# Small array tiles for a linear-attention state, and two vector steps moved to GpSimd

## The chip, the cores and the metric

The kernel runs on one NeuronCore of one Trainium2 chip. A core has engines that run their own instruction queues side by side: TensorE (PE, with its weight loads PEld) for matrix products, VectorE (DVE), ScalarE (ACT), GpSimd (POOL), and SyncE (SP), which issues DMA transfers here. On-chip operands lie in SBUF; matrix products land in PSUM. The metric is the device time of one launch in microseconds, lower is better. Arrays are f32 at the interface.

## The reference

Four layers run one after the other on x of 2048 tokens by 512 columns, each as x + layer(layernorm(x)): layers 1 and 3 are softmax attention with 32 heads of 16 columns, layers 2 and 4 a linear attention with learned features ("hedgehog"). Both kinds use the same weights in both places.

```
def _B_ref(x, wqkv, w_phi, wo):
    qkv = (x @ wqkv).reshape(B, S, 3, H, Dh) ...
    pq = einsum("bhsd,hdf->bhsf", q, w_phi)
    pk = einsum("bhsd,hdf->bhsf", k, w_phi)
    phi_q = concatenate([softmax(pq), softmax(-pq)], axis=-1)
    phi_k = concatenate([softmax(pk), softmax(-pk)], axis=-1)
    kv  = einsum("bhsf,bhsd->bhfd", phi_k, v)
    z   = einsum("bhsf->bhf", phi_k)
    num = einsum("bhqf,bhfd->bhqd", phi_q, kv)
    den = einsum("bhqf,bhf->bhq", phi_q, z)[..., None] + 1e-6
    return (num / den).transpose(0, 2, 1, 3).reshape(B, S, D) @ wo
```

So in a linear layer every head has 32 features per token (16 from softmax(p), 16 from softmax(-p)), and a state of 32 x 17: 16 columns of v and one of ones, which gives the denominator. Here S = 2048, H = 32, Dh = 16.

## The kernel before, in words

Two classes hold the layers: `LayerA` (softmax) and `LayerB` (linear). The program is layer 1 (`a1`), 2 (`b1`), 3 (`a2`), 4 (`b2`). Weights are folded and split into two f16 parts once, beside layer 1, and kept in DRAM. Tokens go in four blocks `j` of 512, each of four tiles `t` of 128. A further path for very large scores (`LayerAny`) stands behind a branch that is not taken.

A linear layer has three stages. In `feed` (L1051), for each of the 16 token tiles, PE makes pk, pq and the values in PSUM (36 matmuls of 128x512, L1064). `expo` (L1119) takes the maximum and the minimum per head (L1124, L1125), writes x - max and min - x side by side into `f` (L1127, L1128), all on DVE, and ACT takes the exponential of both (L1129). `part_sums` (L1132) forms the inverse row sums on DVE (L1135, L1136, L1138), and `share` (L1141) multiplies by them on Pool (L1144). For k, `halves` (L1146) splits the result into two f16 parts: ACT the high one (L1150), Pool the low one (L1151). PE adds the tile's product of features and values to the state in `gather` (L1178). For q, `turn` (L1169) transposes on PE and copies by ACT. The value tile `vt` is a new buffer for each token tile, with two memsets on Pool (L1068, L1069). Tiles 0 to 9 of a linear layer also carry the end of the softmax layer before it: pieces of its output projection, its residual sums, the statistics of the next norm (small Pool instructions, L406 to L423), and one norm step a tile (L446, L456, L459).

When the last tile is in, `blocks` (L1186) copies the state from PSUM into `kvb`: two tiles of 4 groups of 128 columns, zero apart from four 32x17 blocks on the diagonal of each group. `heads(j)` (L1198) multiplies it with the transposed features of a block: 8 f32 matmuls of 128x128 against 512 tokens (L1204), two groups in each double bank of PSUM. `norm2` (L525) brings each double bank out: ACT copies (L528), DVE transposes in 32x32 blocks (L530), DVE adds the small constant and inverts (L532, L533), DVE multiplies (L535), and `finish_o` (L516) transposes back on DVE (L518), ACT takes the high half (L522), Pool the low half (L523). `rest` runs heads 0 and 1; `finish` (L1215) runs the output projection (L559, L585), the residual sum (L575), heads 2 and 3 and, in layer 2, the first part of layer 3.

Who sets the order: within `feed` of the linear layer all compute engines follow the program as written; in `rest` and `finish` DVE, ACT and Pool, and in layer 4's `finish` PE also, stand in an order that a planner makes from its own costs. SyncE's queue is ordered by the planner everywhere. PSUM has three double banks under the name "S" (one holds the state during `feed`) and two single banks.

Layers 1 and 3 begin with octet 0 of the heads; the weights of octet 1 are loaded by `octet_w` (L624). In L272 to L274 and L809 to L811 this stands ahead of `load_head`, which loads the row operands for the first scores; `feed_end` (L825) loads the remaining rows and the shift row.

Of the kernel before, what the change touches and what calls it, by code (L numbers as in the profile page):

```python
# [50 lines left out]
def mha_hedgehog_stack(ctx, tc, x_in, a_wqkv, a_wo, b_wqkv, b_wphi, b_wo, out, shmin=SHMIN):  # L51
# [14 lines left out]
    def big(shape, dt, name):  # L66
        return bigp.tile(shape, dt, tag="big", name=name)
# [94 lines left out]
    def prep_a():  # L162
# [38 lines left out]
        with tc.manual_schedule(engines=COMPUTE):  # L201
            a1.begin((w0, v0))
            ln.stats(0, 2, True)
            ln.stats(2, 2, True)
            mk = [peak_of(flat(wk), 0, nc.scalar)]
            ln.scaled(0), ln.scaled(1)
            ps01, ps23 = bank2(), bank2()
            ln.transposed(0, 2, ps01)
            mk += [peak_of(flat(wk), 1, nc.scalar), peak_of(flat(wq), 0, nc.scalar), peak_of(flat(wq), 1, nc.vector)]
            ln.scaled(2), ln.scaled(3)  # L210
            ln.high(0, 2, ps01)
            ln.transposed(2, 2, ps23)
            ln.high(2, 2, ps23)
            es, sc = scale_from(mk, "sA")
            con["scA"] = sc
            high0(w0[:, :, 1], wk, sc), high0(w0[:, :, 0], wq, sc)
            stats1 = lns[1].stats_parts(0, 4)
            next(stats1)
            low0(w0[:, :, 1], wk, sc)
            run(stats1)  # L220
            low0(w0[:, :, 0], wq, sc)
            con["qk"] = cp.tile([P, 1], F32, name="c_qk")
            nc.vector.tensor_scalar(con["qk"], es, QS / 8192.0, None, op0=ALU.mult)
            con["q1"] = cp.tile([P, 1], F32, name="c_q1")
            nc.vector.tensor_scalar(con["q1"], es, 1.0 / 8192.0, None, op0=ALU.mult)
            ln.low(0, 2, ps01)
            ln.low(2, 2, ps23)
            mv = [peak_of(flat(wv), u, nc.scalar) for u in range(2)]
            pj = {ten: bank2()[:, 0, :] for ten in (1, 0)}
            gens = {ten: a1.project(0, 0, pj[ten], ten) for ten in (1, 0)}  # L230
            for ten in (1, 0):
                for _ in range(4):
                    next(gens[ten])
            run(gens[1]), run(gens[0])
            lns[1].scaled(0), lns[1].scaled(1)
            con["esA"], con["scAv"] = scale_from(mv, "sAv")
            high0(v0, wv, con["scAv"])
            lns[1].scaled(2), lns[1].scaled(3)
            a1.head_evac(0, 1, pj[1])
            low0(v0, wv, con["scAv"])  # L240
            a1.head_evac(0, 0, pj[0], False)
            nc.sync.dma_start(dA[0], w0)
            nc.sync.dma_start(dAv[0], v0)
            for j in range(1, NJ):
                ln = lns[j]
                ps01, ps23 = bank2(), bank2()
                ln.transposed(0, 2, ps01)
                ln.transposed(2, 2, ps23)
                ln.high(0, 2, ps01)
                ln.high(2, 2, ps23)  # L250
                a1.head_square(j - 1, 0)
                if j == 1:
                    lns[2].stats(0, 4)
                ln.low(0, 2, ps01)
                ln.low(2, 2, ps23)
                if j < NJ - 1:
                    a1.head_values(j - 1)
                nxt = [lambda t=t: lns[j + 1].scaled(t) for t in range(4)] if j + 1 < NJ else []
                if j == 1:
                    octet(1)  # L260
                for f in nxt:
                    f()
                if j > 1:
                    octet(j)
                if j == 2:
                    a1.head_norms(0)
                a1.head(j, (1,))
                if j + 2 < NJ:
                    lns[j + 2].stats(0, 4)
                a1.head(j, (0,), j == NJ - 1)  # L270
                octet_low(j)
                if j == 2:  # L272
                    a1.next_w = a1.octet_w(1)
                    a1.load_head()  # L274
            a1.feed_end()

# [71 lines left out]
    def prep_rest():  # L348

        yield from prep_ao()  # L350
        while len(folded) < 2:
            yield
        es, sc = scale_from((yield from peaks(folded)), "sB")
        con["pB"] = cp.tile([P, 1], F32, name="c_pB")
        nc.vector.tensor_scalar(con["pB"], es, 1.0 / 8192.0, None, op0=ALU.mult)
        for i in range(2):
            yield from split_parts(folded[i], sc, f"bhl{i}", dBqk[:, i])
        wv = load_w(b_wqkv[:, 1024:1536], "bwv")
        yield from landing()
        esv, scv = scale_from((yield from peaks([wv])), "sBv")  # L360
        yield from split_parts(wv, scv, "bhlv", *[dBv[a] for a in range(2)])

        wo = big([P, NC4, 512], F32, "bwo")
        for h in range(4):
            for q in range(2):
                r = h * 32 + q * DH
                nc.sync.dma_start(wo[r:r + DH], b_wo.rearrange("(c q h d) n -> q h d c n", q=2, h=4, d=DH)[q, h])
        yield from landing()
        eso, sco = scale_from((yield from peaks([wo])), "sBo")
        yield from split_parts(wo, sco, "bhlo", dBo)  # L370
        con["oB"] = out_scale(esv, eso, "c_oB")
# [153 lines left out]
    def norm2(ps, dst):  # L525

        raw = pp.tile([P, 2 * 512], F32, tag="p", name="raw")
        nc.scalar.activation(raw, ps.rearrange("p q t -> p (q t)"), AF.Copy)  # L528
        yt = pp.tile([P, 2, 16, 32], F32, tag="p", name="yt2")
        nc.vector.transpose(yt.rearrange("p q a b -> p (q a b)"), raw)  # L530
        rec = sp.tile([P, 2, 16], F32, name="rec2", bufs=2)
        nc.vector.tensor_scalar(rec, yt[:, :, :, 16], 1e-6 * KS, None, op0=ALU.add)  # L532
        nc.vector.reciprocal(rec, rec)  # L533
        yn = np_.tile([P, 16, 32], F32, tag="yn", name="yn2", bufs=5)
        nc.vector.tensor_tensor(yn.rearrange("p a (q d) -> p q a d", q=2), yt[:, :, :, 0:16],  # L535
                                rec.unsqueeze(3).to_broadcast([P, 2, 16, 16]), ALU.mult)
        finish_o(yn, dst)

# [77 lines left out]
    class LayerA:  # L616
# [179 lines left out]
        def feed(self, lns, work):  # L796

            for j, (a, b, c) in enumerate(work):
# [8 lines left out]
                    self.head_norms(0)  # L807
                self.head(j)
                if j == 2:  # L809
                    self.next_w = self.octet_w(1)  # L810
                    self.load_head()  # L811
                if 0 < j < NJ - 1:
                    self.head_values(j - 1)
# [11 lines left out]
        def feed_end(self):  # L825
            self.head_norms(1)
            self.head_bound(2)
            self.load_shift(0, slice(0, AHEAD), None, (1,))
            self.load_rows(0, slice(AHEAD, S), self.kq_end)
            self.head_values(2)  # L830
            self.head_norms(2)
            self.head_bound(3)
# [202 lines left out]
    class LayerB:  # L1035
# [3 lines left out]
        def begin(self):  # L1039
# [6 lines left out]
                self.wv.append(t)  # L1046
            self.kvp = None
            self.latek = self.lateq = None
            self.qT, self.obs = [], []

        def feed(self, j, xnT, between=lambda t: None):  # L1051

# [4 lines left out]
            for t in range(4):  # L1057
# [6 lines left out]
                            nc.tensor.matmul(dst, xnT[:, a, c, t * P:(t + 1) * P], w(b, c),  # L1064
                                             start=(i == 0 and c == 0), stop=(i == 2 and c == NC4 - 1))

                vt = np_.tile([P, 2, H, 17], F16, tag="yn", name="vt", bufs=5)
                nc.gpsimd.memset(vt[:, 0, :, 16:17], 1.0)  # L1068
                nc.gpsimd.memset(vt[:, 1, :, 16:17], 0.0)  # L1069
                bank = lambda name: psS.tile([P, 2, 512], F32, tag="S", name=name)[:, 0, :]  # L1070
                last = tt == NT - 1
                pk = bank("pk")
                project(pk, lambda b, c: self.wqk[:, 1, b, c, :])
                if last:
                    f_k = self.expo(pk)
                    self.kvb = [np_.tile([P, 4, P], F32, tag="yn", name="kvb", bufs=5) for _ in range(2)]
                    for kvb in self.kvb:
                        nc.gpsimd.memset(kvb, 0.0)
                else:
                    pq = bank("pq")  # L1080
                    project(pq, lambda b, c: self.wqk[:, 0, b, c, :])
# [37 lines left out]
        def expo(self, ps):  # L1119
# [5 lines left out]
            nc.vector.tensor_reduce(mn, pf, AX.X, ALU.min)  # L1125
            f = pp.tile([P, H, 2, DH], F32, tag="p", name="f")
            nc.vector.tensor_tensor(f[:, :, 0, :], pf, mx.unsqueeze(2).to_broadcast([P, H, DH]), ALU.subtract)  # L1127
            nc.vector.tensor_tensor(f[:, :, 1, :], mn.unsqueeze(2).to_broadcast([P, H, DH]), pf, ALU.subtract)  # L1128
            nc.scalar.activation(f, f, AF.Exp, scale=con["pB"])  # L1129
            return f  # L1130

# [53 lines left out]

        def blocks(self):  # L1186

            for i, kvb in enumerate(self.kvb):
                for h in range(4):
                    r = 32 * h  # L1190
                    dst = kvb[r:r + 32, :, r:r + 17]
                    src = self.kvp[r:r + 32, i, 0:272].rearrange("p (g e) -> p g e", g=4)[:, :, h * 17:h * 17 + 17]
                    if i:
                        nc.scalar.activation(dst, src, AF.Copy)
# [1 line left out]
                        nc.vector.tensor_copy(dst, src)  # L1196

        def heads(self, j):  # L1198
            ob = big([P, NC4, 2, 512], F16, f"obB{j}")
            for o in range(4):  # L1200
                ps = psS.tile([P, 2, 512], F32, tag="S", name="pn")
                for par in range(2):
                    g = 2 * o + par
                    nc.tensor.matmul(ps[:, par, :], self.kvb[g // 4][:, g % 4, :], self.qT[j][g // 4][:, g % 4, :], start=True, stop=True)  # L1204
                norm2(ps, ob[:, o])
            self.obs.append(ob)

        def rest(self):
# [193 lines left out]
```

## Time and profile before

| what | us |
|---|---|
| median of three runs | 2550.31 |
| lowest and highest run | 2549.44, 2551.63 |
| the profiled execution | 2549.26 |
| its span in the trace | 2547.5 |
| PE busy | 2447.8 |
| ACT busy | 2177.5 |
| DVE busy | 974.0 |
| POOL busy | 379.0 |

The profile is of one execution. Rows of the page and of the groups give line, engine, operation, output and inputs, shapes and count, then busy time, mean ns of one, and the engine's idle time just before with what ended it. Rows in order of time begin with the start and the length in us from the start of the span. L1144 is line 1144 of the kernel before. The granted clock of the profiled execution was 0.99 of full speed.

### The profile page before, as it was taken

What the parts mean: (1) busy time and instruction counts of PE and PEld (TensorE: products, weight loads), DVE (VectorE), ACT (ScalarE), POOL (GpSimd) and SP (SyncE); (2) the same over time, 40 slices, a digit from 0 to 9 for tenths busy, and PEclk for the clock granted to TensorE, in tenths of its full rate; (3) what the DMA queues carried; (4) which work ended last, traced back from release to release, by engine and by line L of the source; (5) the groups of instructions that cost most, each with busy time, mean ns of one, the idle gap of its engine ahead of it and who ended that gap; (6) DMA issues with size and microseconds to landing.
All of it is one profiled execution on the core that took longest, in us unless ns stands there. A gap on an engine that the chain in (4) does not pass through costs nothing.

```text
span 2547.5 us, 50724 instructions
## 1 busy us (share of the span) xinstructions
PE 2447.8 (96%) x20960; PEld 761.2 (30%) x20960; DVE 974.0 (38%) x1884; ACT 2177.5 (85%) x2437; POOL 379.0 (15%) x523
## 2 busy tenths in 40 slices
PE   6799999999999999999899999999999999998998
PEld 3222222222232222345343222222222222224543
DVE  6212211212133316899871122112122111459897
ACT  5699999999999999644438999999999999993552
POOL 2100000101000000266430010000010000005552
PEclk9899999999999999999999999999999999999999
DMA  3510230033033612100224003202300351110003
GB/s 141 104 44 5 43 47 6 14 50 78 1 79 66 222 51 84 50 17 6 70 96 68 14 6 50 40 1 45 65 2 10 71 140 41 67 67 26 9 17 109
DMA packets 109650, 135.29 MB, mean 53 GB/s; under 512 B 63408, under 2 KB 64672, under 8 KB 107232
## 3 DMA queue, kind: packets, MB, share of 16 engines
q1 hardware_dynamic: 108736, 129.59, 20.7%
q8 instruction: 166, 2.72, 0.4%
q0 software_dynamic: 672, 2.36, 0.2%
q14 instruction: 76, 0.62, 0.1%
HBM read 60.06 MB, written 39.85 MB: 39 GB/s over the span
## 4 chain that ended last, share of the span: by engine, by line
PE 78%; DVE 11%; ACT 5%; issue 3%; POOL 2%; SPq 1%; DMA 0%; ACTq 0%; POOLq 0%; DVEq 0%
PE pv L891 37%; PE s L877 21%; PE pqk L585 6%; PE po L585 5%; ACT p L880 3%; DVE su L1135 2%; PE pbv L1064 1%; PE pk L1064 1%; PE pq L1064 1%; DVE f L1127 1%; POOL f L1144 1%; DVE f L1128 1%; DVE mx L1124 1%; PE pst L446 1%; DVE su L1136 1%
## 5 line engine op out<-in xcount | busy, mean ns | idle before, releaser
L880 ACT ACTIVATE p<-s 128x1024 f32<-128x1024 f32 x2048 | 1887.8, 1116 | 20.2 <-PE s L877 17.7
L891 PE MATMUL pv<-p,v 128*32 128x512 f32 x8192 | 1091.9, 605 | 2.6 <-DVE yt L503 1.8
L877 PE MATMUL s<-kq 49*128 49x512 f16 x3872 | 606.1, 382 | 20.3 <-DMA kq<-sh 12.0
L877 PEld LDWEIGHTS <-kq 49*128 49x128 f16 x3968 | 136.8, 94 | 637.4 <-issue 625.3
L891 PEld LDWEIGHTS pv<-p,v 128*32 128x32 f32 x8192 | 161.8, 108 | 397.3 <-issue 367.2
L687 POOL TENSOR_TENSOR sq<-stg 128x512 bf16<-128x512 f16 x48 | 70.1, 1460 | 1043.1 <-DVE stg L761 940.2
L503 DVE STREAM_TRANSPOSE yt<-pv 128x512 f32<-128x512 f32 x64 | 45.8, 716 | 452.9 <-PE pv L891 441.0
L760 DVE TENSOR_SCALAR tq<-pqk,c_qk 128x512 f32<-128x512 f32 x48 | 35.9, 749 | 445.0 <-PE pqk L585 411.8
L1144 POOL TENSOR_TENSOR f<-f,su 128x1024 f32<-128x1024 f32 x62 | 119.8, 1933 | 386.0 <-DVE su L1138 351.6
L1064 PEld LDWEIGHTS <-xnTa 128*128 128x128 f16 x1152 | 110.6, 99 | 150.8 <-DVE f L1128 23.6
L585 PEld LDWEIGHTS <-wA 128*32 128x32 f16 (+1 forms) x2496 | 86.6, 97 | 200.8 <-issue 175.2
L573 DVE SCALAR_TENSOR_TENSOR xt<-po,c_oA,xt 128x512 f32<-128x512 f32 x64 | 47.1, 735 | 233.9 <-PE po L585 223.5
L585 PE MATMUL pqk<-xnTb,wA 128*32 128x512 f16 (+1 forms) x1248 | 116.9, 379 | 2.2 <-ACT xnTb L456 2.2
L585 PE MATMUL pqk<-xnT,wA 128*32 128x512 f16 (+1 forms) x1224 | 110.9, 379 | 3.1 <-ACT xnT L456 2.5
L1064 PE MATMUL pbv<-wbv,xnTa 128*128 128x512 f16 x384 | 92.9, 394 | 19.0 <-DVE f L1128 19.0
L1129 ACT ACTIVATE f<-f,c_pB 128x1024 f32<-128x1024 f32 x64 | 72.7, 1148 | 42.3 <-DVE f L1128 42.2
L1150 ACT ACTIVATE fk<-f 128x1024 f16<-128x1024 f32 x30 | 31.7, 1057 | 73.6 <-POOL f L1144 73.6
L585 PE MATMUL po<-woA,ob 128*32 128x512 f16 x1152 | 92.3, 379 | 0.0
L1064 PE MATMUL pk<-wbqk,xnTa 128*128 128x512 f16 x384 | 88.5, 379 | 0.0
L1064 PE MATMUL pq<-wbqk,xnTa 128*128 128x512 f16 x384 | 88.4, 379 | 0.0
L1135 DVE TENSOR_REDUCE su<-f 128x64 f32<-128x1024 f32 x64 | 77.5, 1211 | 9.2 <-ACT f L1129 8.5
L1176 ACT ACTIVATE qT<-pqt 128x512 f32<-128x512 f32 x64 | 34.6, 593 | 52.0 <-PE pqt L1175 52.0
(280 smaller groups left out, 1930.1 us busy)
## 6 DMA issues: line engine op xcount, KB each, us to landing
kq<-stg SPq DMA_DIRECT2D x168, 128.0 KB
xd<-xt SPq DMA_DIRECT2D x40, 512.0 KB
xt<-xd SPq DMA_DIRECT2D x40, 512.0 KB
v<-vyt SPq DMA_DIRECT2D x384, 16.0 KB
oD<-osp SPq DMA_DIRECT2D x24, 256.0 KB
ob<-oD SPq DMA_DIRECT2D x8, 768.0 KB
xt<-in_A_x_dram SPq DMA_DIRECT2D x8, 512.0 KB
wbqk<-dBqk SPq DMA_DIRECT2D x2, 2048.0 KB
```

The costliest lines, as they stand in the source:

```text
L503: nc.vector.transpose(yt.rearrange("p a b -> p (a b)"), ps)
L573: nc.vector.scalar_tensor_tensor(xt[:, u, :], ps, co, xt[:, u, :], op0=ALU.mult, op1=ALU.add)
L585: nc.tensor.matmul(ps[r, :], w[:, r], x, start=(n == 0), stop=(n == of - 1), skip_group_check=cols)
L687: nc.gpsimd.tensor_tensor(sq, hi, hi, ALU.mult)
L760: nc.vector.tensor_scalar(tq, ps, cqk, CLAMP, op0=ALU.mult, op1=ALU.min)
L877: nc.tensor.matmul(s[:, u, :], self.side(g, half, r, 0, kt * P, P), self.side(g, half, r, 1, j * 512, 512), start=True, stop=True)
L880: nc.scalar.activation(pt, s, AF.Exp, scale=0.25 / (QS * QS))
L891: nc.tensor.matmul(acc[32 * hh:32 * hh + 32, :], self.oct[o]["v"][:, r:r + 32], pt[:, hh % 2, :], start=(kt == 0), stop=(kt == NT - 1), sk ...
L1064: nc.tensor.matmul(dst, xnT[:, a, c, t * P:(t + 1) * P], w(b, c), start=(i == 0 and c == 0), stop=(i == 2 and c == NC4 - 1))
L1129: nc.scalar.activation(f, f, AF.Exp, scale=con["pB"])
L1135: nc.vector.tensor_reduce(su, f[:, r, :], AX.X, ALU.add)
L1144: nc.gpsimd.tensor_tensor(f3, f3, self.part_sums(f3, slice(0, 64), factor), ALU.mult)
```

## The change

Five edits stand together.

1. The state is kept as 8 groups of 32 columns in one `kvb` tile, not as diagonal blocks. `heads` takes the features in two halves; each half is 16 matmuls of a 32x32 array tile, a different one for each, written to two double banks of PSUM at once. The order of heads that comes out is another, so the rows of `wo` are loaded in that order, by 16 transfers in place of 8.
2. min - x is formed on Pool in two steps: min - max of 32 columns, then that minus (x - max), which DVE has written to SBUF.
3. The product with the inverse sums in `norm2` is on Pool.
4. The value tiles rotate over three buffers, whose constant columns are written once per layer.
5. The call that loads the next octet's weights is moved out of the loops and into `feed_end`, behind the rows' loads.

```diff
@@ prep_a, LayerA.feed
                 if j == 2:
-                    a1.next_w = a1.octet_w(1)
                     a1.load_head()
@@ feed_end
             self.load_rows(0, slice(AHEAD, S), self.kq_end)
+            self.next_w = self.octet_w(1)
             self.head_values(2)
@@ prep_rest
-        for h in range(4):
-            for q in range(2):
-                r = h * 32 + q * DH
-                nc.sync.dma_start(wo[r:r + DH], b_wo.rearrange("(c q h d) n -> q h d c n", q=2, h=4, d=DH)[q, h])
+        for i in range(4):
+            for c in range(4):
+                r = 32 * c + DH * (i % 2)
+                nc.sync.dma_start(wo[r:r + DH, i // 2:4:2, :],
+                                  b_wo.rearrange("(k h d) n -> h d k n", k=2, d=DH)[4 * ((c - i) % 4) + i])
@@ norm2
-        nc.vector.tensor_tensor(yn.rearrange("p a (q d) -> p q a d", q=2), yt[:, :, :, 0:16],
+        nc.gpsimd.tensor_tensor(yn.rearrange("p a (q d) -> p q a d", q=2), yt[:, :, :, 0:16],
                                 rec.unsqueeze(3).to_broadcast([P, 2, 16, 16]), ALU.mult)
@@ LayerB.feed
-                vt = np_.tile([P, 2, H, 17], F16, tag="yn", name="vt", bufs=5)
-                nc.gpsimd.memset(vt[:, 0, :, 16:17], 1.0)
-                nc.gpsimd.memset(vt[:, 1, :, 16:17], 0.0)
+                if tt < 3:
+                    self.vts.append(np_.tile([P, 2, H, 17], F16, tag="yn", name="vt", bufs=5))
+                    nc.gpsimd.memset(self.vts[tt][:, 0, :, 16:17], 1.0)
+                    nc.gpsimd.memset(self.vts[tt][:, 1, :, 16:17], 0.0)
+                vt = self.vts[tt % 3]
...
-                    self.kvb = [np_.tile([P, 4, P], F32, tag="yn", name="kvb", bufs=5) for _ in range(2)]
-                    for kvb in self.kvb:
-                        nc.gpsimd.memset(kvb, 0.0)
+                    self.kvb = np_.tile([P, 8, 32], F32, tag="yn", name="kvb", bufs=5)
+                    nc.gpsimd.memset(self.kvb, 0.0)
@@ expo
             nc.vector.tensor_tensor(f[:, :, 0, :], pf, mx.unsqueeze(2).to_broadcast([P, H, DH]), ALU.subtract)
-            nc.vector.tensor_tensor(f[:, :, 1, :], mn.unsqueeze(2).to_broadcast([P, H, DH]), pf, ALU.subtract)
+            nc.gpsimd.tensor_tensor(mn, mn, mx, ALU.subtract)
+            nc.gpsimd.tensor_tensor(f[:, :, 1, :], mn.unsqueeze(2).to_broadcast([P, H, DH]), f[:, :, 0, :], ALU.subtract)
@@ blocks
-                    dst = kvb[r:r + 32, :, r:r + 17]
+                    dst = self.kvb[r:r + 32, 4 * i:4 * i + 4, 0:17]
@@ heads
-            for o in range(4):
-                ps = psS.tile([P, 2, 512], F32, tag="S", name="pn")
-                for par in range(2):
-                    g = 2 * o + par
-                    nc.tensor.matmul(ps[:, par, :], self.kvb[g // 4][:, g % 4, :], self.qT[j][g // 4][:, g % 4, :], start=True, stop=True)
-                norm2(ps, ob[:, o])
+            for k in range(2):
+                ps = [psS.tile([P, 2, 512], F32, tag="S", name="pn") for _ in range(2)]
+                for g in range(4):
+                    for i in range(4):
+                        c = 32 * ((i + g) % 4)
+                        r = slice(32 * i, 32 * i + 32)
+                        nc.tensor.matmul(ps[i // 2][c:c + 32, i % 2, :], self.kvb[r, 4 * k + g, :],
+                                         self.qT[j][k][r, g, :], start=True, stop=True, skip_group_check=True)
+                for p in range(2):
+                    norm2(ps[p], ob[:, 2 * k + p])
```

More of the change, by code (lines that the diff above doesn't have):

```diff
@@ L809, in feed @@
                 if j == 2:
-                    self.next_w = self.octet_w(1)
                     self.load_head()
@@ L1048, in begin @@
             self.latek = self.lateq = None
-            self.qT, self.obs = [], []
+            self.qT, self.obs, self.vts = [], [], []
         def feed(self, j, xnT, between=lambda t: None):
@@ L1186, in blocks @@
         def blocks(self):
-            for i, kvb in enumerate(self.kvb):
+            for i in range(2):
                 for h in range(4):
                     r = 32 * h
-                    dst = kvb[r:r + 32, :, r:r + 17]
+                    dst = self.kvb[r:r + 32, 4 * i:4 * i + 4, 0:17]
                     src = self.kvp[r:r + 32, i, 0:272].rearrange("p (g e) -> p g e", g=4)[:, :, h * 17:h * 17 + 17]
```

## The prediction, made before the result was known

> **What bounds the kernel now.** I read the page first, then tables of stretches for the two linear layers, then one token tile in order of time, the groups of instructions, and the chain that ended last. In every row of a group the last two numbers are busy us and mean ns, then idle time.
>
> ```profile
> span 2547.5 us, 50724 instructions
> PE 2447.8 (96%) x20960; PEld 761.2 (30%) x20960; DVE 974.0 (38%) x1884; ACT 2177.5 (85%) x2437; POOL 379.0 (15%) x523
> ```
>
> The averages mislead. The two softmax layers, some 2,000 us, are not touched: in the built program their PE instructions stand in the same order. All that changes lies in the linear layers: layer 2 from about 1047 to 1348 us, layer 4 from 2297 to the end. I call the moment at which DVE starts the first row sum of token tile t (su, L1135) its mark. The table cuts layer 2 at the marks of tiles 0, 1, 2, 3, 4, 5, 9, 14 and 15, and adds the stretch of the first normalisations. Columns: length, then busy us and count of PE, PEld, DVE, ACT, POOL.
>
> ```profile
> 1052.62:1062.23 9.61, 8.81 (x51) 4.17 (x44) 9.51 (x16) 4.81 (x6) 6.28 (x5) 1.00 0.00 0
> 1062.23:1078.17 15.94, 13.19 (x105) 6.68 (x104) 13.15 (x22) 6.24 (x9) 8.98 (x19) 0.89 0.12 45
> 1078.17:1087.78 9.61, 9.40 (x63) 4.55 (x60) 9.51 (x15) 4.67 (x6) 6.28 (x5) 1.00 0.10 37
> 1087.78:1101.06 13.28, 10.51 (x77) 5.28 (x76) 13.04 (x23) 4.92 (x6) 9.38 (x20) 0.89 0.11 41
> 1101.06:1111.40 10.34, 10.34 (x73) 5.52 (x71) 9.28 (x15) 4.95 (x7) 6.27 (x5) 0.98 0.00 0
> 1111.40:1155.83 44.43, 40.46 (x291) 22.53 (x290) 38.52 (x61) 22.98 (x30) 25.06 (x20) 1.00 0.04 13
> 1155.83:1202.54 46.71, 46.65 (x335) 24.76 (x334) 45.16 (x72) 22.86 (x28) 31.37 (x25) 1.00 0.00 1
> 1202.54:1209.92 7.38, 6.27 (x51) 3.13 (x49) 5.04 (x9) 3.87 (x5) 4.04 (x3) 1.00 0.13 36
> 1216.00:1246.00 30.00, 27.88 (x101) 12.58 (x100) 29.82 (x52) 15.92 (x24) 11.59 (x11) 1.00 0.10 36
> ```
>
> Tiles 9 to 13 are plain: PE is busy 46.65 of 46.71 us, 9.34 us a tile. Tiles 5 to 8 also carry a piece of the norm; they take 11.11 us, and neither PE nor DVE is full. In the last row DVE is full. One tile of the 11.11 us kind:
>
> ```profile
> 1122.52 1.21 DVE L1135 TENSOR_REDUCE su<-f 128x64 f32<-128x1024 f32 x1
> ...
> 1124.35 0.20 DVE L1138 TENSOR_SCALAR su<-su 128x64 f32<-128x64 f32 x1
> ...
> 1124.69 1.93 POOL L1144 TENSOR_TENSOR f<-f,su 128x1024 f32<-128x1024 f32 x1 [4.43 <-DVE su L1138]
> ...
> 1126.65 1.06 ACT L1150 ACTIVATE fk<-f 128x1024 f16<-128x1024 f32 x1 [2.39 <-POOL f L1144]
> ...
> 1127.03 1.94 POOL L1144 TENSOR_TENSOR f<-f,su 128x1024 f32<-128x1024 f32 x1 [0.41 <-DVE su L1136]
> 1127.62 0.58 ACT L456 ACTIVATE xnTa<-pst 128x512 f16<-128x512 f32 x1
> ...
> 1128.23 0.69 DVE L459 TENSOR_TENSOR xnTa<-pst,xnTa 128x512 f16<-128x512 f32 x1 [1.37 <-ACT xnTa L456]
> ...
> 1128.92 2.13 POOL L1151 TENSOR_TENSOR fk<-f,fk 128x1024 f16<-128x1024 f32 x1
> ...
> 1130.03 0.68 DVE L1127 TENSOR_TENSOR f<-pk,mx 128x512 f32<-128x512 f32 x1
> 1130.63 0.68 DVE L1128 TENSOR_TENSOR f<-mn,pk 128x512 f32<-128x512 f32 x1
> ...
> 1131.34 1.15 ACT L1129 ACTIVATE f<-f,c_pB 128x1024 f32<-128x1024 f32 x1 [0.36 <-DVE f L1128]
> ...
> 1133.62 1.21 DVE L1135 TENSOR_REDUCE su<-f 128x64 f32<-128x1024 f32 x1
> ```
>
> The loop: row sums (DVE), share of k (POOL), high half (ACT), norm copy (ACT, DVE), then four DVE steps on the next tile's k, exponential (ACT), next mark. Pool's three instructions of the tile are in order; the last ends 1131.05, 8.53 us behind the mark. Nothing of the next tile needs Pool until its own mark, so this end is harmless today.
>
> **The change part by part.**
>
> ```profile
> L1144 POOL TENSOR_TENSOR f<-f,su 128x1024 f32<-128x1024 f32 x62 | 119.8, 1933 | 386.0 <-DVE su L1138 351.6 <-DVE su L1136 28.5 <-PE po L585 5.9
> L1204 PE MATMUL pn<-qT,kvb 128*128 128x512 f32 x128 | 59.5, 610 | 8.2 <-ACT raw L528 6.0 <-DVE xt L575 1.5 <-DVE kvb L1196 0.7
> L523 POOL TENSOR_TENSOR obB<-yb,obB 128x512 f16<-128x512 f32 x32 | 37.2, 1162 | 68.2 <-ACT obB L522 68.2
> L535 DVE TENSOR_TENSOR yn<-yt,rec 128x512 f32<-128x512 f32 x32 | 26.4, 824 | 0.0
> L1128 DVE TENSOR_TENSOR f<-mn,pq 128x512 f32<-128x512 f32 x32 | 21.7, 677 | 0.0
> L406 POOL TENSOR_TENSOR lu<-ly 128x2 f32<-128x2 f32 x36 | 8.3, 231 | 21.5 <-DVE ly L397 19.1
> ```
>
> min - x. DVE loses 64 instructions of 0.68 us; Pool gets 64 pairs: min - max over 128x32, then the difference over 128x512. Between Pool's 231 ns for 2 elements and 1,933 ns for 1,024 lies 1.67 ns an element, so 0.28 us and 1.08 us, together 1.37. Half of 1,933 is the lower end for the large one, 0.97; the other Pool instruction of 512 elements, 1.16, the upper; I take 1.08.
>
> What counts is the place. The pair for k feeds ACT's exponential and stands in Pool's queue behind the previous tile's three instructions. So the next mark cannot come before 8.53 (queue free) + 1.37 (the pair) + 1.15 and some 0.05 (exponential) = 11.1 us. In a plain tile that replaces PE's 9.34: the stall moves from PE to Pool, and DVE and PE wait. Even at no length for the pair the floor is 9.73. In a tile with a norm piece DVE's x - max ends at about 8.2 (its row ends at 8.19), so Pool's 8.53 is last and the tile stays 11.1: what DVE sheds is not on the path.
>
> Layer 2 by marks: 0 to 1, 9.61 to 11.1 (+1.5); 2 to 3 the same (+1.5); 4 to 5, 10.34 to 11.1 (+0.8); 5 to 9 none; 9 to 14, 46.71 to 55.5 (+8.8). Into tile 4 Pool first finishes the norm's small statistics:
>
> ```profile
> 1099.93 0.19 POOL L423 TENSOR_TENSOR lb<-lu,ly 128x2 f32<-128x2 f32 x1
> ```
>
> From its end 1100.12 the pair and the exponential give 1102.7 for a mark that was at 1101.06 (+1.6). Into tile 2 the statistics hold ACT as well; 0, at most the same 1.6. Tile 14 has no second share: high half done at 5.2, low half 2.13, pair and exponential: 9.95 for 7.38 (+2.6). Sum +16.8, twice +33.6; with the ends of the pair 31 to 37.
>
> Memsets of vt fall from 64 to 12; they ran on Pool while it idled: 0. Fewer kvb columns: 0.
>
> The multiplication by the inverse sums. DVE loses 16 x 0.82 us a layer, Pool gets about 16 x 1.08, placed between DVE's reciprocal and DVE's second transpose, so both engines take turns within a tile. In the stretch from 1216 DVE falls from 29.8 by 8 x 0.82 + 0.68 to 22.6 us, Pool rises from 11.6 by 8 x 1.08 + 1.37 to 21.6. That could give 7 us. But DVE waits for a running Pool instruction in one place here:
>
> ```profile
> 1222.12 1.93 POOL L1144 TENSOR_TENSOR f<-f,su 128x1024 f32<-128x1024 f32 x1 [6.84 <-DVE su L1136]
> ...
> 1223.03 1.06 DVE L532 TENSOR_SCALAR rec<-yt 128x32 f32<-128x32 f32 x1
> ...
> 1225.82 0.11 DVE L532 TENSOR_SCALAR rec<-yt 128x32 f32<-128x32 f32 x1
> ```
>
> The same 32-column instruction takes 0.11 us with Pool idle and 1.06 when Pool runs, until just past Pool's end (1224.05). With Pool twice as full, some of the eight wait about 1 us each. I take 0, ends -7 and +8. The Trainium skill, GPSIMD Engine Reference, Key points, says that Pool shares its SBUF interfaces with VectorE and meets it in two-port modes and with two SBUF inputs; by that rule every such step behind a Pool instruction waits, which is the third rival, and the trace agrees with this 1.06.
>
> The array tiles. A half of heads() was four matmuls, now 16 of 32x32.
>
> ```profile
> L891 PE MATMUL pv<-p,v 128*32 128x512 f32 x8192 | 1091.9, 605 | 2.6 <-DVE yt L503 1.8 <-DVE ly L397 0.3
> L1182 PE MATMUL kvp<-vt,fk 128*128 128x68 f16 x768 | 30.2, 194 | 4.4 <-POOL fk L1151 2.4 <-DVE fk L1166 1.3 <-ACT fk L1165 0.4
> ```
>
> Each f32 matmul is two records, 59.5/128 = 0.46 us each, so a half is 3.7 us. Four column tiles run side by side (1091.9/2048 = 0.53 for four records). No row shows 16: at best 0.93 a half, at worst four groups of four, 3.7. Short matmuls issue every 30.2/768 = 39 ns, 32 records in 1.3 us; I take 1.3. The Trainium skill, TensorEngine Tiling (Array Packing), Tiling Modes, counts 16 independent 32x32 tiles; by that a half would be the 0.93. Each half now holds two of three double banks at once, so the second waits for one ACT copy of about 1.0 us: heads() is about 3.7 us in place of 7.
>
> ```profile
> 2496.47 5.42 PE pn L1204 x12
> 2501.89 10.36 PE po L585 x48
> 2512.25 6.87 PE pn L1204 x16
> 2519.12 20.73 PE po L585 x96
> 2539.88 1.28 DVE xt L575
> ```
>
> At the end of layer 4 both heads() lie on the chain: 5.42 and 6.87 lose some 5. Yet the normalised result of the last heads() had 6.87 + 10.36 us of PE as cover and now has 14; four normalisations, each about 3 us through DVE and Pool in turn, then come last by 1 us or so. I take -4, ends -8 and +2. In layer 2 the chain also goes through the statistics and ACT: -3, ends -8 and +5.
>
> The permuted rows of wo are 16 smaller loads for 8 in attention, 240 us ahead of their use: 0. The next octet's weights: in the built program both loads stand in SyncE's queue exactly where they stood, ahead of the row loads in layer 1 and beside wbo in layer 3, with the same waits. This part does nothing: 0.
>
> Sum: +33.6 + 0 - 3 - 4 = +26.6 on the profiled execution's 2549.3 us, 1 us below the median: 2576.
>
> **Rivals.** First, faster: the smaller matmuls pay everywhere. 59.5 us of pn become 16 x 1.3 = 21; were all on the path, 38.7 come back and the time is 2544. It decides from the point where more than 33.6 come back. For it: pn on the last chain; against: DVE is full where half of them run. Second, the 32x32 tiles run only four at a time: heads() is 7.4 plus two bank waits, 9.5; the end of each layer loses some 7 us against my sum: 2590. Third, DVE waits behind Pool in most of the 32 normalisations: 1 us each in the 16 that DVE paces gives 16, 2592.
>
> **How the numbers follow.** Forecast 0.60, first rival 0.12, second 0.13, third 0.15. Faster by over 0.2% (5 us, about what a measurement here can tell from none) 0.12; within it 0.04, the forecast's low edge; slower 0.84. The range 2557 to 2596 holds the forecast with its ends and the two slow rivals, and leaves the fast one out.
>
> **What would show it.** Marks of tiles 9 to 14 near 11.1 us apart, Pool busy 8.7 us of each, ACT's exponential released by Pool's new line, PE idle some 1.7 us a tile. Tiles 5 to 8 unchanged. A half of pn near 1.3 us. The tensor_scalar L532 longer than 0.24 us on average. It is wrong if Pool's large difference takes under 0.9 us, or if the plain tiles stay below 10 us.

## The result and the profile after

The changed kernel takes 2585.81 us (median of four runs, 2584.94 to 2586.22) beside 2549.88 us for the kernel before: a ratio of 1.0141, 95% interval 1.0129 to 1.0154. That is slower by 36 us. The forecast was 2576 us, in a range of 2557 to 2596; its sign and its main cause held, and it fell 10 us short. From the page of the changed kernel:

```profile
span 2583.1 us, 51562 instructions
PE 2451.1 (95%) x21344; PEld 749.7 (29%) x21344; DVE 918.8 (36%) x1788; ACT 2181.4 (84%) x2437; POOL 483.0 (19%) x629
```

DVE lost 55 us of work and Pool gained 104. The table by stretches answers to that of the kernel before: it is cut at the marks (the starts of the first row sum, here L1137) of tiles 0, 1, 2, 3, 4, 5, 9, 14 and 15 of layer 2, with 30 us of the first normalisations last. Behind the five engines each row ends with PE's granted clock, the busy share of the DMA engines and GB/s.

```profile
1052.00:1063.64 11.64, 10.88 (x89) 5.59 (x92) 8.49 (x13) 4.93 (x6) 9.16 (x10) 1.00 0.00 0
1063.64:1079.60 15.96, 12.41 (x88) 5.76 (x80) 11.95 (x19) 6.25 (x9) 11.49 (x24) 0.89 0.15 52
1079.60:1090.69 11.09, 10.29 (x84) 5.28 (x80) 8.40 (x14) 4.79 (x6) 8.37 (x7) 1.00 0.06 23
1090.69:1105.60 14.91, 11.46 (x63) 5.02 (x56) 11.98 (x19) 4.93 (x6) 11.61 (x23) 0.89 0.10 36
1105.60:1116.69 11.09, 10.48 (x94) 5.96 (x91) 7.78 (x13) 4.93 (x6) 8.50 (x8) 1.00 0.01 1
1116.69:1161.01 44.32, 40.14 (x271) 21.14 (x270) 34.10 (x53) 23.07 (x30) 33.95 (x29) 1.00 0.04 13
1161.01:1216.41 55.40, 49.89 (x363) 25.86 (x360) 38.86 (x61) 23.58 (x28) 42.49 (x36) 1.00 0.00 1
1216.41:1226.37 9.96, 6.44 (x47) 2.98 (x46) 4.36 (x7) 3.87 (x5) 5.70 (x6) 0.91 0.27 105
1232.45:1262.45 30.00, 21.98 (x179) 7.53 (x178) 24.35 (x42) 16.07 (x24) 20.04 (x20) 0.85 0.10 37
```

The plain tiles 9 to 13 went from 46.71 to 55.40 us, 11.08 a tile, and PE is no longer full there: it idles 1.1 us of each, where I expected 1.7; Pool is busy for 8.5. Tiles 5 to 8 did not change (44.43 and 44.32). In the last row the granted clock is 0.85, where it was 1.00. One plain tile in order of time:

```profile
1183.17 1.22 DVE L1137 TENSOR_REDUCE su<-f 128x64 f32<-128x1024 f32 x1 [3.21 <-ACT f L1131]
...
1185.35 1.94 POOL L1146 TENSOR_TENSOR f<-f,su 128x1024 f32<-128x1024 f32 x1 [2.06 <-DVE su L1140]
...
1187.66 1.93 POOL L1146 TENSOR_TENSOR f<-f,su 128x1024 f32<-128x1024 f32 x1 [0.37 <-DVE su L1138]
...
1188.57 0.68 DVE L1128 TENSOR_TENSOR f<-pk,mx 128x512 f32<-128x512 f32 x1
...
1189.55 2.14 POOL L1153 TENSOR_TENSOR fk<-f,fk 128x1024 f16<-128x1024 f32 x1
...
1191.65 0.25 POOL L1129 TENSOR_TENSOR mn<-mn,mx 128x32 f32<-128x32 f32 x1
1191.98 1.06 POOL L1130 TENSOR_TENSOR f<-mn,f 128x512 f32<-128x512 f32 x1
...
1193.07 1.15 ACT L1131 ACTIVATE f<-f,c_pB 128x1024 f32<-128x1024 f32 x1 [1.64 <-POOL f L1130]
...
1194.25 1.22 DVE L1137 TENSOR_REDUCE su<-f 128x64 f32<-128x1024 f32 x1 [3.21 <-ACT f L1131]
```

DVE has x - max ready at 1189.25. Pool begins the low half of the tile before at 1189.55 and reaches the pair at 1191.65, 8.48 us behind the mark. Exponential and mark follow, and DVE has then waited 3.21 us. The groups that carry the costs:

```profile
L1131 ACT ACTIVATE f<-f,c_pB 128x1024 f32<-128x1024 f32 x64 | 73.4, 1150 | 88.0 <-POOL f L1130 88.0
L1130 POOL TENSOR_TENSOR f<-mn,f 128x512 f32<-128x512 f32 x64 | 67.7, 1057 | 7.2 <-DVE f L1128 2.5
L1210 PE MATMUL pn<-qT,kvb 32*32 32x512 f32 x512 | 35.4, 723 | 17.5 <-ACT raw L528 9.8 <-DVE xnTb L459 5.8 <-DVE xt L575 1.6
L1129 POOL TENSOR_TENSOR mn<-mn,mx 128x32 f32<-128x32 f32 x64 | 16.2, 253 | 258.1 <-DVE mn L1126 257.8
L532 DVE TENSOR_SCALAR rec<-yt 128x32 f32<-128x32 f32 x32 | 9.3, 292 | 0.1
```

The rest of a linear layer (from the mark of tile 15 to the first matmul of heads(2)) and the end of layer 4, in the kernel before and then in the changed one:

```profile
1209.92:1245.47 35.55, 32.35 (x164) 15.71 (x165) 33.75 (x57) 18.52 (x29) 14.83 (x17) 1.00 0.14 53
2458.89:2494.44 35.55, 32.35 (x164) 15.75 (x164) 33.76 (x57) 18.51 (x29) 14.66 (x15) 1.00 0.08 30
2494.44:2547.50 53.06, 45.24 (x177) 19.88 (x175) 34.50 (x49) 13.85 (x17) 11.57 (x10) 0.95 0.38 131
```

```profile
1226.37:1266.36 39.99, 30.17 (x233) 11.81 (x231) 32.00 (x55) 19.29 (x30) 25.24 (x24) 0.85 0.09 34
2494.37:2536.02 41.65, 34.09 (x229) 13.27 (x228) 31.20 (x50) 19.38 (x30) 25.14 (x22) 0.71 0.10 33
2536.02:2583.10 47.08, 37.61 (x273) 15.06 (x272) 27.02 (x39) 12.60 (x16) 17.32 (x16) 0.96 0.42 141
```

The difference of the two spans adds up from these marks: start -0.6, tiles of layer 2 +17.1, its rest +4.4, from there to layer 4 -3.5, tiles of layer 4 +18.1, its rest +6.1, the end -6.0; 35.6 us. In this execution of the kernel before, one tile of layer 2 came 1 us late (mark 4 to 5, 10.34 us, where layer 4 has 9.33), so that layer's +17.1 stands for some +18.1.

### The profile page after: what moved, and what is told of

The parts are those of the page before. It is cut to its first block, busy times and chain, and to the rows that moved or that the text cites. A ratio compares the mean times of both kernels' runs of the same rounds, so it can differ in the third digit from the quotient of the medians.

```text
span 2583.1 us, 51562 instructions
## 1 busy us (share of the span) xinstructions
PE 2451.1 (95%) x21344; PEld 749.7 (29%) x21344; DVE 918.8 (36%) x1788; ACT 2181.4 (84%) x2437; POOL 483.0 (19%) x629
## 4 chain that ended last, share of the span: by engine, by line
PE 73%; DVE 10%; POOL 7%; ACT 6%; issue 3%; SPq 1%; DMA 0%; POOLq 0%; ACTq 0%; DVEq 0%
PE pv L891 37%; PE s L877 21%; PE pqk L585 5%; PE po L585 5%; ACT p L880 3%; DVE su L1137 3%; POOL f L1146 2%; POOL fk L1153 2%; ACT f L1131 1%; POOL f L1130 1%; DVE su L1138 1%; PE pst L446 1%; DVE vt L1093 1%; DVE st L389 1%; POOL yn L535 1%
## 5 line engine op out<-in xcount | busy, mean ns | idle before, releaser
L760 DVE TENSOR_SCALAR tq<-pqk,c_qk 128x512 f32<-128x512 f32 x48 | 35.9, 749 | 445.2 <-PE pqk L585 445.2
L1137 DVE TENSOR_REDUCE su<-f 128x64 f32<-128x1024 f32 x64 | 77.8, 1215 | 83.3 <-ACT f L1131 83.3
L585 PE MATMUL po<-wbo,obB 128*128 128x512 f16 x336 | 75.1, 382 | 0.4 <-POOL obB L523 0.4
```

The lines of the kernel that those rows point to most:

```text
L585: nc.tensor.matmul(ps[r, :], w[:, r], x, start=(n == 0), stop=(n == of - 1), skip_group_check=cols)
L1137: nc.vector.tensor_reduce(su, f[:, r, :], AX.X, ALU.add)
```

## The experiments

All times are medians; "tiles" is the time from the mark of tile 0 to that of tile 15, "rest" as above, each in layers 2 and 4, read from the traces.

| kernel | median us | ratio to before, 95% | tiles | rest |
|---|---|---|---|---|
| before | 2549.9 | | 157.3, 156.3 | 35.6, 35.6 |
| changed | 2585.8 | 1.0141 (1.0129 to 1.0154) | 174.4, 174.4 | 40.0, 41.7 |
| 1, min - x back on DVE | 2540.3 | 0.9968 (0.9957 to 0.9980) | 156.3, 156.3 | 36.5, 36.4 |
| 2, before, min - x on Pool | 2590.6 | 1.0161 (1.0144 to 1.0178) | 175.9, 176.1 | 36.1, 35.9 |
| 3, multiplication back on DVE | 2578.7 | 1.0115 (1.0098 to 1.0132) | 174.2, 174.2 | 37.3, 36.7 |
| 4, both back on DVE | 2544.4 | 0.9983 (0.9974 to 0.9993) | 156.3, 156.3 | 36.9, 35.2 |
| 5, low half later | 2574.2 | 1.0096 (1.0080 to 1.0111) | 170.0, 169.8 | 40.6, 38.0 |
| 6, pair for q alone | 2546.9 | 0.9985 (0.9976 to 0.9994) | 160.5, 159.3 | 35.9, 37.2 |
| 7, PE filled | 2546.7 | 0.9987 (0.9978 to 0.9997) | 157.5, 156.3 | 34.0, 34.1 |
| 8, before, multiplication on Pool | 2551.6 | 1.0011 (1.0002 to 1.0021) | 156.3, 157.7 | 35.9, 35.9 |
| 9, Pool work off the loop | 2580.7 | 1.0124 (1.0106 to 1.0143) | 174.2, 174.2 | 39.6, 39.5 |
| 10, Pool work on the loop | 2619.6 | 1.0277 (1.0259 to 1.0296) | 191.9, 191.9 | 40.0, 41.7 |
| 11, last q on DVE | 2576.3 | 1.0109 (1.0094 to 1.0125) | 174.2, 174.2 | 36.4, 37.1 |
| 12, copy first | 2530.0 | 0.9923 (0.9910 to 0.9937) | 150.9, 150.6 | 36.1, 36.2 |

In some executions one tile of the first five is about 1 us late (157.3, 157.5 and 157.7 in the table, against 156.3). Experiments 9 and 10 ran in two timed runs each.

**1 to 4: one move at a time.** Experiment 1 undoes the second edit:

```diff
-            nc.gpsimd.tensor_tensor(mn, mn, mx, ALU.subtract)
-            nc.gpsimd.tensor_tensor(f[:, :, 1, :], mn.unsqueeze(2).to_broadcast([P, H, DH]), f[:, :, 0, :], ALU.subtract)
+            nc.vector.tensor_tensor(f[:, :, 1, :], mn.unsqueeze(2).to_broadcast([P, H, DH]), pf, ALU.subtract)
```

> The changed kernel with min - x back on DVE as in the kernel before; all other edits stay. Theory (place in Pool's queue): the pair behind the low half is what stretched the 16 tiles of each linear layer, 17.1 us in layer 2 and 18.1 us in layer 4 between the marks of tiles 0 and 15. Without it marks 9 to 14 are 9.34 us apart again and the time is 2585.8 - 35 = 2551 us, 2547 to 2553. Rival: the value tiles that rotate over three buffers, or the clock that the small matmuls leave behind, carry part of the stretch: plain tiles stay above 10 us and the time above 2560.

Experiment 2 makes the reverse edit alone in the kernel before.

> The kernel before with min - x on Pool as the only edit. Theory: the whole stretch of the tiles appears alone: marks 9 to 14 11.1 us apart and 2549.9 + 35 = 2585 us, 2582 to 2590 (the memsets of the value tiles, 0.24 us each, are still in Pool's queue and may add up to 0.5 us a tile, 16 us in all, if they stand ahead of the pair). Rival: the pair costs only together with the other edits: under 2570.

Experiment 3 undoes the third edit, and experiment 4 the second and the third.

```diff
-        nc.gpsimd.tensor_tensor(yn.rearrange("p a (q d) -> p q a d", q=2), yt[:, :, :, 0:16],
+        nc.vector.tensor_tensor(yn.rearrange("p a (q d) -> p q a d", q=2), yt[:, :, :, 0:16],
```

> The changed kernel with the multiplication by the inverse sums back on DVE. Between the mark of tile 15 and heads(2) the changed kernel is 4.4 us longer in layer 2 and 4.1 us in layer 4. Theory: the multiplication on Pool is the cause, DVE and Pool take turns and ACT's copies behind them free PSUM late: these 8.5 us go, 2577 us. Rival 1: the pair for the last q and a lower granted clock of TensorE carry them, and the multiplication on Pool spares DVE 16 x 0.82 = 13 us a layer of which some pays: 2586 to 2592. Feed marks unchanged in both.

> The changed kernel with both moves to Pool undone: what is left is the small array tiles, the order of the rows of wo, the three value tiles and the moved load. Theory: heads() at 3.5 us in place of 7 pays where heads 2 and 3 lie on the chain; from heads(2) on the changed kernel gained 6.4 us in layer 2 and 4.3 us in layer 4, and DVE paces the rest as before: 2549.9 - 5 to - 10, 2540 to 2545 us. Rival: with DVE full in the rest and in the normalisations of finish nothing of it pays: 2548 to 2552.

The tiles settle the first question. With min - x on DVE they take 156.3 us, with the pair on Pool 174 to 176, whatever else stands in the kernel. From experiment 1, the same stretches (marks 5 to 9, marks 9 to 14):

```profile
1109.01:1153.42 44.41, 40.46 (x291) 22.53 (x290) 38.51 (x61) 22.90 (x30) 23.82 (x12) 1.00 0.04 13
1153.42:1200.14 46.72, 46.66 (x335) 24.74 (x334) 45.16 (x72) 22.86 (x28) 29.79 (x15) 1.00 0.00 1
```

The rotating value tiles cost the tiles nothing; with the memsets still in Pool's queue, where they stand between the low half and the pair, experiment 2 has 11.2 us a plain tile in place of 11.08. But the totals are not sums of parts. The pair cost 34.2 us with the multiplication on DVE (3 less 4) and 45.5 us with it on Pool (changed less 1). The multiplication on Pool gained 4.1 us without the pair (1 less 4) and lost 7.1 us with it (changed less 3). Experiment 3 came within 2 us of its theory: its rests are 2.7 and 4.9 us shorter than the changed kernel's, though the pair is still on Pool. In experiment 1 they are 3.5 and 5.2 us shorter, though the multiplication is still on Pool. So it takes both moves together to lengthen the rests by this much. Experiment 1 was 7 us below its range, mostly because the rests came back too; experiment 2 ended 0.6 us above its own. The small tiles and the lesser parts (4) are worth 5 us, as expected.

**5, 9 and 10: place in the queue or amount of work.** Experiment 5 moves the low half behind the next pair for k:

```diff
                     f_k = self.expo(pk)
+                    if self.latek is not None:
+                        self.low_half(*self.latek)
+                        self.gather(*self.latek)
                     f_q = self.expo(pq)
```

> The changed kernel with one instruction moved in Pool's queue: the low half of a tile's k features (2.13 us) is issued behind the next tile's pair for k, not ahead of it, and the product of features and values is issued after it; the same Pool work in all, 8.7 us a tile. Theory (place in the queue decides, not the amount): Pool is free for the pair at mark + 6.4 in place of 8.5, so the pair and the exponential allow a next mark at 6.4 + 1.37 + 1.15 = 8.95, TensorE's 9.34 binds again or TensorE waits a little for the late low half: marks 9 to 14 between 9.34 and 10.0 us apart, time 2585.8 - 2 x (10 to 17) = 2552 to 2566 us. Rival (amount of Pool work, or Pool slowing DVE while both run): the period stays at 11.1 and the time at 2583 to 2588.

The gather's call moves with it, and `low_half` holds the last line of `halves`. The plain tiles came to 10.9 us, between my bounds and the rival's and nearer the rival's; the time of 2574 us lies midway between the two ranges. The first row sum of q now starts 4.2 us behind that of k, where it was 2.55. The low half that no longer delays the pair for k delays the pair for q, and with it the share of q, behind which the next pair for k stands: another loop through the same queue, which I had not drawn. So it decides nothing, and experiments 9 and 10 were made to decide. Both issue the same four added instructions a tile, at two places:

```diff
+                    for _ in range(4):
+                        nc.gpsimd.tensor_tensor(dum, self.mq[0], self.mq[1], ALU.subtract)
```

> The changed kernel with four more Pool instructions a tile (min - max over 128x32 into a tile that nobody reads, 0.25 us each, some 1.0 us together), in Pool's queue behind the pair for q and ahead of the next share of k. There Pool is idle for 2.0 us a tile in the changed kernel. Theory (Pool's queue is on the loop only from the share of k to the pair): plain tiles stay at 11.1 us, Pool's busy time a tile rises from 8.7 to 9.7 us and the time stays at 2584 to 2588 us. Rival (the amount of Pool work, or what DVE loses while Pool runs, sets the period): 1.0 us more a tile, 15 tiles in two layers, 2616 us.

> The same four added Pool instructions, but in the queue between the low half and the pair for the next tile's k. Theory: each nanosecond ahead of the pair lengthens the loop: 12.1 us a plain tile, 14 or 15 tiles in two layers, 2585.8 + 28 to 33 = 2614 to 2619 us. Rival: the pair is not what releases the next mark; the tile has slack there: under 2600 us.

Marks 9 to 14 in experiment 9, and then in experiment 10:

```profile
1159.69:1215.05 55.36, 49.88 (x363) 25.81 (x360) 38.86 (x60) 23.54 (x28) 47.26 (x56) 1.00 0.00 1
```

```profile
1171.62:1232.99 61.37, 50.01 (x342) 25.38 (x341) 38.87 (x60) 23.54 (x28) 47.26 (x56) 1.00 0.00 1
```

Pool's work is the same in both, 47.26 us. Behind the pair for q and ahead of the next share it costs nothing (55.36, as in the changed kernel); ahead of the pair each tile is 1.20 us longer, for four instructions that take 1.24, and the time is 2619.6 us (2614 to 2619 expected). The place decides, not the amount, and DVE's own busy time does not grow with Pool's.

Experiment 9 is 5 us faster than the changed kernel though it does more, and 3 us below its range. Of the 5 us, 2.2 are the rest of layer 4, at a clock of 0.83 against 0.71. Differences of this size between single builds are therefore not read from totals here, but from marks.

**6: the pair for q alone.**

```diff
-        def expo(self, ps):
+        def expo(self, ps, pool=False):
...
-                    f_q = self.expo(pq)
+                    f_q = self.expo(pq, True)
```

The argument says whether min - x is on Pool.

> The changed kernel with min - x of k, and of the last tile's q, on DVE; the pairs for the q of tiles 0 to 14 stay on Pool. The exponential of q is needed 2.5 us behind the mark, not at it, so this pair is off the loop. Theory: plain tiles stay at 9.34 us; in the run with min - x all on DVE the marks of tiles 5 to 9 are set by DVE's eighth step of 0.60 us (it ends as the first row sum starts), so the seven left give 10.5 us a tile there, and some 4 us less a layer: 2540.3 - 8 = 2532 us, 2528 to 2537. Rival: any pair in Pool's queue delays the next share and lengthens plain tiles: above 2540 us.

Marks 5 to 9, and 9 to 14:

```profile
1113.92:1155.95 42.03, 40.52 (x288) 21.98 (x287) 36.49 (x56) 22.70 (x30) 28.53 (x20) 1.00 0.04 14
1155.95:1203.88 47.93, 47.12 (x334) 24.56 (x332) 42.22 (x66) 23.08 (x28) 35.77 (x24) 1.00 0.00 1
```

Tiles 5 to 8 take 10.5 us, as worked out, so DVE's eighth step was on that loop. The plain tiles lose 0.25 us each, and tiles 0 to 4 lose more: tile 0 to 1 went from 9.61 to 10.38 us. The tiles together are 3 to 4 us longer than in experiment 1, and the whole is 6.6 us slower. So the rival has the right time, but not the reason in the plain tiles, for Pool waits there before the share of k:

```profile
1168.53 1.93 POOL L1149 TENSOR_TENSOR f<-f,su 128x1024 f32<-128x1024 f32 x1 [1.65 <-DVE su L1143]
```

The delay runs through ACT instead. The exponential of q waits 0.60 us for the pair, ACT's copy of the values stands behind it, DVE waits 0.20 us for that copy, and the first row sum of q starts 2.84 us behind the mark, not 2.55.

**11: which part of the rest.**

```diff
-                    self.todo = [self.lateq, (tt, self.expo(pq), qT)]
+                    self.todo = [self.lateq, (tt, self.expo(pq, False), qT)]
```

Here the same argument is true by default.

> The changed kernel with min - x on DVE for the q of the last tile only, which stands in the rest, beside the normalisations. From the mark of tile 15 to heads(2) the changed kernel takes 40.0 us in layer 2 and 41.7 us in layer 4; with all of min - x on DVE it takes 36.5 us in both. Theory A (Pool has the pair, two shares and the multiplications at once): 36.5 us again in both layers, 2585.8 - 8.5 = 2577 us. Theory B (the last tiles' wait for Pool leaves TensorE idle and its granted clock at 0.50 into the rest): 39 us or more stays, 2583 to 2586 us.

Theory A: 9.5 us come back, and 8.1 of them lie in the two rests. Where, is seen in ACT's order behind the last q. The changed kernel, layer 4:

```profile
2518.78 1.03 ACT L528 ACTIVATE raw<-pn 128x1024 f32<-128x1024 f32 x1 [0.62 <-PE pn L1210]
2519.70 0.62 ACT L522 ACTIVATE obB<-yb 128x512 f16<-128x512 f32 x1
2521.18 0.63 ACT L522 ACTIVATE obB<-yb 128x512 f16<-128x512 f32 x1 [0.87 <-DVE yb L518]
2521.72 2.83 ACT L528 ACTIVATE raw<-pn 128x1024 f32<-128x1024 f32 x3
```

Experiment 11:

```profile
2511.76 0.63 ACT L522 ACTIVATE obB<-yb 128x512 f16<-128x512 f32 x1 [1.03 <-DVE yb L518]
2512.29 1.92 ACT L528 ACTIVATE raw<-pn 128x1024 f32<-128x1024 f32 x2
2514.10 0.63 ACT L522 ACTIVATE obB<-yb 128x512 f16<-128x512 f32 x1
2514.62 1.02 ACT L528 ACTIVATE raw<-pn 128x1024 f32<-128x1024 f32 x1
```

With the pair on Pool the planner puts three of the four copies of heads(1) behind the last transposed result of heads(0), which comes through Pool; without it, two stand behind the third and one behind the fourth. PE's output projection (L559) needs a bank that such a copy frees: it starts 28.4 us behind the mark in the changed kernel and 25.3 us in experiment 11, although the exponential of the last q starts only 0.66 us later. That the pair brings this about is shown. How much of it is the new order and how much the clock (0.71 and 0.82 in this rest) is not separated.

**7: the clock in the rest.** The base is experiment 1.

```diff
+                if (j, k) == (1, 0):
+                    for _ in range(2):
+                        nc.tensor.matmul(psum1("warm"), ident, self.qT[j][k][:, 0, :], start=True, stop=True)
```

> The changed kernel with min - x on DVE, and two more f32 matmuls of 128x512 per linear layer (some 1.8 us of TensorE, written to a bank that nobody reads), in the 2.3 us for which TensorE idles inside the second heads() of the rest. There the granted clock falls to 0.50 for 7 us, and the first 24 matmuls of the output projection take 7.8 us where the kernel before takes 5.7. Theory (the idle time brings the clock down, and that costs the chain): the clock stays at 1.00, the 24 take 5.7, and 2540.3 - 4 = 2536 us. Rival: the normalisations set the end of this stretch whatever the matmuls do: 2539 to 2542 us. The planner orders DVE, ACT and Pool anew around the added matmuls, so the length of the 24 is the first thing to read.

PE in experiment 1 (layer 2, then layer 4), and in experiment 7:

```profile
1228.93 1.69 PE L1209 MATMUL pn<-qT,kvb 32*32 32x512 f32 x16 [2.26 <-ACT raw L528]
1231.11 7.80 PE L559 MATMUL po<-wbo,obB 128*128 128x512 f16 x24 [0.48 <-ACT raw L528]
...
2493.40 10.53 PE L585 MATMUL po<-wbo,obB 128*128 128x512 f16 x48
```

```profile
1228.41 1.98 PE L1213 MATMUL warm<-qT,ident 128*128 128x512 f32 x4
...
1233.98 5.34 PE L559 MATMUL po<-wbo,obB 128*128 128x512 f16 x24 [1.04 <-ACT raw L528]
...
2496.35 4.36 PE L1209 MATMUL pn<-qT,kvb 32*32 32x512 f32 x60 [1.77 <-DVE xt L575]
2500.64 12.67 PE L585 MATMUL po<-wbo,obB 128*128 128x512 f16 x48
```

The mechanism is right: 24 matmuls take 5.34 us in place of 7.80, and both rests are 2.4 us shorter. The time is wrong: 2546.7 us, above the rival's range too. In layer 4 the matmuls of heads(2) wait longer for DVE's residual sum (1.77 us, 0.31 in experiment 1), and the next 48 matmuls take 12.67 us in place of 10.53: the low clock came later instead (0.50 from 2498.2 to 2505.0). The stretches behind heads(2) are 5.6 us (layer 2 to layer 4) and 5.8 us (the end) longer than in experiment 1. The planner's other order around the added matmuls may have its part in that; it was not taken apart.

**8: the multiplication alone, in the kernel before.** The edit is the reverse of experiment 3.

> The kernel before with only the multiplication by the inverse sums on Pool. On the small tiles, with min - x on DVE, it was worth 2544.4 - 2540.3 = 4 us. Theory: DVE paces the rest and is relieved by 8 x 0.82 us a layer, so it pays without the small tiles too: 2549.6 - 4 = 2546 us, 2543 to 2548. Rival (my prediction's value): DVE and Pool take turns and it comes out at no change, 2548 to 2551.

The interval, 1.0002 to 1.0021, excludes a gain. The median is 2 us above that of the kernel before: close to the value 0 of the prediction, and far from the 4 us gain taken over from experiments 1 and 4.

**12: a faster kernel.** In the tile of 11.11 us that the prediction shows, DVE waits 1.37 us for ACT's norm copy, which stands behind the high half. The base is experiment 1:

```diff
                     self.todo = self.lateq
-                    self.latek = (tt, self.halves(f_k), vt)
                 else:
                     self.share(f_q, 1.0)
-                    self.latek = (tt, self.halves(f_k), vt)
+                between(tt)
+                self.latek = (tt, self.halves(f_k), vt)
                 self.lateq = (tt, f_q, qT)
-                between(tt)
```

> The changed kernel with min - x on DVE, and the norm step of the softmax layer before (TensorE's transposes, ACT's copy, DVE's difference) issued ahead of the high half of the tile's k features, not behind it. In tiles 5 to 8 DVE waits 1.37 us for that copy, which stands behind the high half on ACT, and then does its eight steps; ACT is idle 2.39 us before the high half. Theory (that wait is on the loop of 11.1 us): the copy runs in ACT's idle time, DVE starts its steps 1.3 us earlier, and tiles 5 to 8 take 9.97 us (TensorE's 9.34 and 0.63 of transposes): 4 x 1.1 a layer, more if tiles 0 to 4 gain too: 2540.3 - 9 to - 16, 2524 to 2532 us. Rival: another step comes last there, the low half or the values: 2537 to 2543 us.

```profile
1109.71:1149.14 39.43, 39.43 (x289) 22.52 (x288) 38.60 (x60) 22.87 (x31) 23.83 (x12) 1.00 0.04 15
1149.14:1195.90 46.76, 46.76 (x336) 24.97 (x335) 45.27 (x70) 22.86 (x28) 29.79 (x15) 1.00 0.00 1
```

Marks 5 to 9 now take 39.43 us, 9.86 a tile, and PE is full in both rows. ACT's copy now stands 2 us ahead of the high half (which starts at 1123.71), and DVE's difference no longer waits for it:

```profile
1121.66 0.60 ACT L456 ACTIVATE xnTa<-pst 128x512 f16<-128x512 f32 x1 [0.53 <-PE pst L446]
```

With 5.5 us less in each linear layer this is the fastest of all: 2530.0 us, 0.9923 of the kernel before.

## Why the prediction was right or wrong

**min - x: right, in mechanism and size.** The period was to be 11.1 us from queue end, pair and exponential; it is 11.08. The pair's large part took 1.06 us (1.08 forecast). Single stretches came out at 14.91 (forecast 13.28 + 1.6), 55.40 (55.5), 44.32 (unchanged) and 9.96 (9.95). Only the step from tile 0 to 1 was longer, 11.64 for 11.1. The term was +33.6 and measured +35.1, or 36.2 against tiles without the late one.

**Tiles 5 to 8: right number, incomplete reason.** I put the old 11.1 us on the chain through k and its exponential. That exponential ended at 1132.49, 1.1 us before the mark at 1133.62; DVE's eighth step, for q, ended last:

```profile
1133.02 0.68 DVE L1128 TENSOR_TENSOR f<-mn,pq 128x512 f32<-128x512 f32 x1
```

Experiment 6 confirms it, and experiment 12 shows that what these tiles take above PE's need hung on ACT's copy.

**The multiplication, taken as 0: here the sum failed.** Alone it costs some 2 us (experiment 8). Beside the last q's pair the loss is larger: the rests grew by 4.4 and 6.1 us, and experiment 11 gives 9.5 us back for that pair alone. My step counted the pair as 1.37 us more of Pool's busy time. It left out that the rest is ordered by a planner, and that a small instruction can put ACT's copies into another order, for whose banks PE then waits; the granted clock then averaged 0.85 and 0.71 in stretches that had 1.00 before. How the loss divides between order and clock stays open.

**heads(): right where nothing holds its matmuls.** A half of 16 small matmuls then takes 1.14 us (1.3 forecast, 3.7 were they four at a time). heads(2) of layer 4 in the changed kernel:

```profile
2536.02 1.14 PE L1210 MATMUL pn<-qT,kvb 32*32 32x512 f32 x32
2537.47 2.07 PE L1210 MATMUL pn<-qT,kvb 32*32 32x512 f32 x32 [0.31 <-DVE xt L575]
```

This call takes 3.5 us and heads(3) behind it 3.8. The other six take 6.6 to 9.8 us, because their matmuls wait or stand between other work of PE; in the rests that is about as long as before (7.1 to 9.0). The end of layer 4 behind heads(2) gained 6.0 us, from there in layer 2 to layer 4 3.5 us; forecast were 4 and 3. With the small tiles alone (experiment 4) it is 4.5 and 1.2 us. The second stretch holds the whole of layer 3 and differs by 3 us between experiments 11 and 12 (1052.7 and 1056.0 us), so its gain is no clean measure. By the rule of the Trainium skill, TensorEngine Tiling (Array Packing), Tiling Modes, a half would be 0.93, an estimate; the 1.14 of the trace lies between that and my 1.3.

**Memsets, rows of wo, weights moved: 0, as forecast.** The tiles of experiments 1 and 4 equal those of the kernel before. The memsets do cost something once the pair stands behind them (experiment 2, 0.12 us a plain tile). The rows and the weights were not run by themselves.

**The rivals.** The fast one (38.7 us back) needed the small matmuls on the path everywhere; experiment 4 gives 5. The 32x32 tiles do run more than four at a time. DVE's wait behind Pool stayed a side matter: L532 rose from 240 to 292 ns on average, 1.7 us in all 32, not 16.

## What to carry to other kernels

Before a step is given to an idle engine, look at where it lands in that engine's in-order queue: what counts is the time from the end of the work ahead of it to whoever waits for it, not the engine's share of busy time. The same 1.2 us of Pool work cost nothing at one place of the tile and 1.2 us a tile at another. Read each loop in order of time, name what ends last, and move that: one norm step issued earlier, so that its copy fills idle time of ACT, won 10 us over experiment 1, where the five edits together lost 36.

## What was not expected of the hardware

PE's granted clock fell to 0.50 after a short rest. In experiment 1, PE idles for 2.26 us before the second half of heads(1) (1226.67 to 1228.93); slices of the trace show the clock at 1.00 until 1229, 0.50 from 1229.5, and 1.00 again from 1236.5, and the 24 matmuls in between took 7.80 us. The Trainium skill, TensorE: Matmul & The Clock Gate, Part 1, tells of a half-rate state behind an idle window of about 3.4 us; the trace agrees on the half rate, but the window need not be idle throughout: in the 3.41 us ahead of the drop (1225.88 to 1229.29) PE was busy for 1.15. With that gap filled in experiment 7, the low clock came at the next gap.
